# Rows of token moments by TensorE, ScalarE normalisation, two more seven-product pairs and a new product order in the first DFT chunk

## The chip, the cores and the metric

The kernel runs on one core of one Trainium2 chip. A core has TensorE (matrix products), VectorE and ScalarE (elementwise work), GpSimd (small work and the issue of one DMA queue) and SyncE, here called SP, which issues most loads. The metric is the device time of one execution in microseconds (us). All data is float32.

## The reference

For x of 2048 tokens by 512 features, the reference normalises each token, mixes it by a Fourier transform over both axes, and gates the result with a GLU:

```python
xn = (x - mean) / sqrt(var + 1e-5)                       # per token
a, b = xn @ hid_re.T, xn @ hid_im.T                      # along features
s = seq_re @ a - seq_im @ b                              # along tokens
g = silu((sigmoid(xn @ w_gate) * (xn @ w_up)) @ w_down)  # F = 1792
out = x + s * g
```

## The kernel before

**Arithmetic.** Each float32 operand is split into a high part (a rounded copy, made by ScalarE, line 72) and a low part (the rest, by VectorE, line 73). Every product is three matmuls, high by high, high by low and low by high (`mm3`, lines 75 to 78), of 128 weight columns by 512 moving columns. Blocks of two by two products are done with seven products instead of eight, as Strassen and Winograd do: sums and differences of the operands are made first, by VectorE (line 124), and the products are numbered 1 to 7.

**Stages.** A start stage normalises and transposes the first 1024 tokens and does block (0,0) directly. Then come 91 units of gate/up work, seven for each of the 13 pairs (half of the tokens h, group of 256 hidden features g) listed in `BLOCKS`: (0,1) is units 0 to 6, (0,2) is 7 to 13, (0,3) is 14 to 20, (0,4) is 21 to 27, and so on. Unit i of a block runs product 1, 5, 2, 6, 7, 4 or 3 of gate and up (12 matmuls into the PSUM banks ga/ua, gb/ub, gc/uc). The b banks are free from the gate of product 2 until the next block's seed. After it, a unit may run one item of the down projection of the block before: in a pair of class `Plain` there are four items of 12 matmuls, at units 1, 3, 4 and 6 of the block; in a pair of class `Seven` there are seven items of six matmuls, one a unit, the last carried into the next block. Each item ends in `gather`: two copies out of PSUM by ScalarE (line 302) and one DMA of 512 KB that adds into DRAM (line 304, GpSimd's queue). Pair (0,0) has class `Ready`, which is `Plain` with operands made in the start stage. `Plain` holds for h = 0 and g below 3. A `Seven` pair needs weight sums and differences (`Down`: four of 256 columns, one more split) and four sums of its activations.

**Then the transform.** Four chunks along the sequence (`seq_units`), each with seven products of four units in the order `ORDER = (1, 5, 6, 3, 7, 2, 4)`; chunk 0 also runs the last eight down items, one behind every second unit. Products 5, 6, 7 and 4 take sums t1, t2, t3 and t4 of the DFT matrix blocks, products 1, 2 and 3 the blocks themselves. Then the transform along features follows (`hidden_units`).

**Order.** Nothing is reordered by a scheduler. A loop over the units (the last lines of the kernel function) emits, for each unit n: the functions registered with `sooner(n, f)`; the loads that the next five units need; the operands (splits) of the next two units; the unit's matmuls; and the functions registered with `after(n, f)`. Every engine runs its own instructions in that order and waits on semaphores for the others. So an operand split is made two units ahead, behind whatever ScalarE or VectorE was given before it.

**Tokens 1024 to 2047.** They are needed both row by row (normalised and stored to `xn_part`) and turned (features on partitions, raw x_t loaded). `norm_a` makes mean and scale of a tile of 128 tokens: bn statistics on VectorE, three small GpSimd steps (lines 166 to 168). `norm_b` applies them on VectorE (line 173). For the turned form, `turned_half` stores means and scales to DRAM (`m_part`, four DMAs in which each element of 4 bytes goes to its own place, line 183), loads them back broadcast to all partitions, and subtracts and multiplies (line 188). `sums_ahead` makes sums ahead of their use and stores them to DRAM (`w_part`, `s_part`, `t_part`); `t_part` holds t1 to t4 of the first block of chunk 0.

SBUF work tiles come from one pool of 54 pages of 4 KB a partition.

Of the kernel before, what the change touches and what calls it, by code (L numbers as in the profile page):

```python
# [15 lines left out]
P = 128  # L16
# [7 lines left out]
SB = 512  # L24
# [4 lines left out]
FIRST_TURNED = 1, 4  # L29
SEVEN_FROM = 3  # L30
SHARED = 4, 5, 6
# [5 lines left out]
def fnet_glu_kernel(ctx: ExitStack, tc: tile.TileContext, x, x_t, c_re, c_im, w_h, w_gu, w_down, out):  # L37
# [22 lines left out]
    nc.scalar.activation(warm, mhalf, AF.Sigmoid)  # L60
    moments = const.tile([P, 2, KH], F32, name="moments")
    m_part = dram.tile([2, 2, SB], F32, name="m_part")
# [5 lines left out]
    s_part = dram.tile([2, 4, P, 4, D // 2], F32, name="s_part")  # L68
    t_part = dram.tile([1, 4, P, 2, SB], F32, name="t_part")

# [84 lines left out]
    st_of = {}  # L155

    def norm_a(i):
# [3 lines left out]
        nc.vector.bn_stats(st, xs[i])  # L161
        nc.vector.bn_aggr(mv, st)
        mean, scale = mv[:, 0:1], rs[:, 1:2]
        if i >= KH:
            mean, scale = (moments[:, m, i - KH : i - KH + 1] for m in range(2))
            nc.gpsimd.tensor_scalar(mean, mv[:, 0:1], 0.0, None, op0=ALU.add)
        nc.gpsimd.tensor_scalar(rs[:, 0:1], mv[:, 1:2], EPS, None, op0=ALU.add)
        nc.gpsimd.tensor_tensor(scale, rs[:, 0:1], mhalf, op=ALU.pow)
        st_of[i] = mean, scale

    def norm_b(i):
# [3 lines left out]
    def turned_half(n, b, at):  # L175

        both = Load(m_part[b].rearrange("m t -> (m t)").partition_broadcast(P).rearrange("p (m t) -> p m t", m=2), [2, SB])
        raw = [Load(x_t[(2 + b) * 2 + j], [2, SB]) for j in range(2)]

        def store():  # L180
            at = slice(b * SB // P, (b + 1) * SB // P)
            for m in range(2):
                nc.gpsimd.dma_start(m_part[b, m].rearrange("(o p) -> p o", p=P), moments[:, m, at])

        def step(j, m):
            v = xraw[1, j, b] = raw[j].load()
            by = both.load()[:, m, :].unsqueeze(1).to_broadcast([P, 2, SB])
            nc.vector.tensor_tensor(v, v, by, op=(SUB, ALU.mult)[m])

        after(n, store)  # L190
        sooner(at[0] - 2, both.load)
        for i in range(4):
            if i % 2 == 0:
                sooner(at[i] - 4, raw[i // 2].load)
            after(at[i], lambda i=i: step(*divmod(i, 2)))
# [482 lines left out]
    def sums_ahead(make, blocks, to, at, ahead):  # L678

        steps = make(*blocks, to)  # L680

        def step(dst, a, b, op, to):
            v = combine(dst(), a.get(), b.get(), op)
            nc.gpsimd.dma_start(to, v)

        for i, v in zip({diffs: (1, 3, 0, 0), sums: (0, 0, 3, 1)}[make], blocks):
            sooner(at[i] - ahead, v.load)
        for i, v in zip(at, steps):
            after(i, lambda v=v: step(*v))
# [20 lines left out]

    ORDER = (1, 5, 6, 3, 7, 2, 4)
    TURNED = (1, 5, 6, 2, 7, 3, 4)
    SLOT = {1: 0, "a": 0, 2: 1, "b": 1, 3: 2, 5: 3, 7: 4, 6: 5, 4: 6}
# [11 lines left out]

    def seq_units(job):
        ops = a_operands()
# [7 lines left out]
        for tc_ in range(NT):  # L735
# [7 lines left out]
            for pp in range(4):  # L743
                b11, b12, b21, b22 = c_blocks(tc_, pp)
                if tc_ == 0 and pp < 1:
                    t1, t3, t2, t4 = (Load(t_part[pp, i], [2, SB]) for i in range(4))
                else:
                    t1 = Value([b11, b12], onto(b11.load, b12.load, ADD, nc.vector))
                    t2 = Value([b22], onto(t1.get, b22.load, ADD, nc.vector))
                    t3 = Value([b22], onto(b12.load, b22.load, ADD, nc.vector))  # L750
                    t4 = Value([b21], onto(t2.get, b21.load, ADD, nc.vector))
# [92 lines left out]

            for k in ORDER:
                for pp in range(4):
# [129 lines left out]
    with tc.manual_schedule():  # L976
# [4 lines left out]
        for h, g in BLOCKS:  # L981
# [3 lines left out]
            if (h, g) == FIRST_TURNED:  # L985
                turned_at = len(units)
            job = block(h, w, made, job, Seven(h, wd, made) if h or g >= SEVEN_FROM else Plain(h, g), g in SHARED)
        for i in range(0, KH, 2):
            a, b = ((2, 9), (4, 10), (7, 12), (8, 14))[i // 2]
            if i >= 4:  # L990
                sooner(a - 4, lambda i=i: fetch(KH + i))
            for j in (i, i + 1):
                after(a, lambda j=j: norm_a(KH + j))
                after(b, lambda j=j: norm_b(KH + j))
                after(b + 1, lambda j=j: store_xn(KH + j))
        n = turned_at
# [77 lines left out]
```

## Time and profile before

| what | value |
|---|---|
| runs | 810.9, 811.6, 815.87 us; median 811.6 |
| profiled execution | 809.47 us |
| its span | 807.6 us |
| granted TensorE clock | 0.999 |
| DMA | 193.62 MB, mean 240 GB/s |

The span runs from the first to the last instruction. In the profile's lines PE is TensorE, PEld its weight loads, DVE VectorE, ACT ScalarE, POOL GpSimd; L76 is line 76. A group's line gives its busy time and the mean length of one instruction, then the engine's idle time before it and what ended that. In the windows, each line gives the stretch, its length, then for PE, PEld, DVE, ACT and POOL the busy time and the count of instructions, the granted clock, the mean busy share of the DMA engines and GB/s. Timelines give start, length, engine, line and operation, with the idle time before it in brackets. Matmuls overlap in TensorE's pipeline, so their lengths add up to more than the time they take, and a few matmul records are missing from the trace.

### The profile page before, as it was taken

To read this page: it belongs to the slowest core of one execution; us is meant where nothing else is said; L and a number is where in the kernel's file an instruction comes from. 1 tells how busy PE (TensorE), PEld (TensorE's weight loads), DVE (VectorE), ACT (ScalarE), POOL (GpSimd) and SP (SyncE) were. 2 spreads that over 40 slices of the span, in tenths; PEclk is the share of its full clock that TensorE was granted. 3 is DMA by queue.
4 is the path that set the end of the run, shared out by engine and by line. 5 is a ranking of instruction groups with operands and counts; after the bars stand their busy time and mean duration, and the time that the engine had idled before them with its cause. 6 is when DMAs were issued, how large, how long until landed. Compare 5 with 4: busy or idle time off the path is not lost.

```text
span 807.6 us, 10288 instructions
## 1 busy us (share of the span) xinstructions
PE 801.0 (99%) x3630; PEld 665.3 (82%) x3630; DVE 639.7 (79%) x803; ACT 496.9 (62%) x761; POOL 150.8 (19%) x222
## 2 busy tenths in 40 slices
PE   9999999999999999999999999999999999999997
PEld 7988888888888888888888888888888888888886
DVE  6897879876776787787798796888888876986946
ACT  4674657777676678778877765445445545536360
POOL 3146321221222222131211100011101210001201
PEclk9999999999999999999999999999999999999999
DMA  8366994987899998989899988277929994799976
GB/s 278 140 225 110 219 263 72 182 159 156 240 253 226 290 295 236 236 199 175 236 294 311 282 294 293 98 284 286 329 85 324 350 389 141 244 337 386 314 254 104
DMA packets 55651, 193.62 MB, mean 240 GB/s; under 512 B 6320, under 2 KB 6576, under 8 KB 55600
## 3 DMA queue, kind: packets, MB, share of 16 engines
q0 software_dynamic: 24624, 85.48, 45.4%
q1 hardware_dynamic: 30896, 107.43, 37.7%
q8 instruction: 28, 0.46, 0.2%
q14 instruction: 23, 0.19, 0.1%
q10 hardware_dynamic: 80, 0.07, 0.0%
HBM read 110.62 MB, written 85.99 MB: 243 GB/s over the span
## 4 chain that ended last, share of the span: by engine, by line
PE 98%; DMA 1%; DVE 0%; ACT 0%; SPq 0%; issue 0%
PE pd L77 7%; PE pd L76 7%; PE pd L78 7%; PE ga L76 6%; PE ga L77 6%; PE ua L77 6%; PE ga L78 6%; PE ua L78 6%; PE ua L76 6%; PE gc L77 4%; PE uc L77 3%; PE gc L78 3%; PE uc L78 3%; PE gc L76 3%; PE uc L76 3%; PE ub L77 3%
## 5 line engine op out<-in xcount | busy, mean ns | idle before, releaser
L73 DVE TENSOR_TENSOR page<-page 128x1024 fp32r<-128x1024 f32 (+1 forms) x351 | 332.4, 976 | 110.3 <-ACT page L72 109.2
L72 ACT ACTIVATE page<-page 128x1024 fp32r<-128x1024 f32 (+1 forms) x351 | 284.2, 857 | 93.6 <-DVE page L124 74.2
L124 DVE TENSOR_TENSOR page<-page 128x1024 f32<-128x1024 f32 (+2 forms) x216 | 188.8, 893 | 0.9 <-DMA page<-in_w_gu_dram 0.3
L302 ACT ACTIVATE page<-pd 128x512 f32<-128x512 f32 x178 | 104.6, 598 | 67.5 <-PE pd L78 54.6
L304 POOL DMA_DIRECT2D g_part<-page x81 | 71.6, 949 | 282.5 <-ACT page L302 166.4
L76 PE MATMUL pd<-page 128*128 128x512 f32 x234 | 91.0, 389 | 0.0
L77 PE MATMUL pd<-page 128*128 128x512 f32 x234 | 91.0, 389 | 0.0
L78 PE MATMUL pd<-page 128*128 128x512 f32 x234 | 91.0, 389 | 0.0
L76 PE MATMUL ga<-page 128*128 128x512 f32 x200 | 78.2, 391 | 0.0
L77 PE MATMUL ga<-page 128*128 128x512 f32 x200 | 77.9, 389 | 0.0
L76 PE MATMUL ua<-page 128*128 128x512 f32 x200 | 77.8, 389 | 0.0
L77 PE MATMUL ua<-page 128*128 128x512 f32 x200 | 77.8, 389 | 0.0
L78 PE MATMUL ga<-page 128*128 128x512 f32 x200 | 77.8, 389 | 0.0
L78 PE MATMUL ua<-page 128*128 128x512 f32 x200 | 77.8, 389 | 0.0
L76 PEld LDWEIGHTS pd<-page 128*128 128x128 f32 x234 | 43.9, 188 | 9.2
L78 PEld LDWEIGHTS pd<-page 128*128 128x128 f32 x234 | 43.9, 188 | 9.1
L77 PEld LDWEIGHTS pd<-page 128*128 128x128 f32 x234 | 43.9, 188 | 9.1
L77 PE MATMUL gc<-page 128*128 128x512 f32 x124 | 48.3, 390 | 0.0
L76 PE MATMUL gc<-page 128*128 128x512 f32 x124 | 48.2, 389 | 0.0
L78 PE MATMUL gc<-page 128*128 128x512 f32 x124 | 48.2, 389 | 0.0
L76 PE MATMUL uc<-page 128*128 128x512 f32 x124 | 48.2, 389 | 0.0
L78 PE MATMUL uc<-page 128*128 128x512 f32 x124 | 48.2, 389 | 0.0
(133 smaller groups left out, 1302.3 us busy)
## 6 DMA issues: line engine op xcount, KB each, us to landing
g_part<-page POOLq DMA_DIRECT2D x89, 512.0 KB, 8.3
page<-f_part SPq DMA_DIRECT2D x36, 512.0 KB, 6.1
page<-in_c_re_dram SPq DMA_DIRECT2D x34, 512.0 KB, 6.2
page<-in_c_im_dram SPq DMA_DIRECT2D x33, 512.0 KB, 7.0
f_part<-page POOLq DMA_DIRECT2D x28, 512.0 KB, 6.9
page<-in_w_gu_dram SPq DMA_DIRECT2D x22, 512.0 KB, 7.0
page<-xn_part SPq DMA_DIRECT2D x14, 512.0 KB, 5.6
page<-in_w_down_dram SPq DMA_DIRECT2D x11, 512.0 KB, 7.9
```

What stands on the lines that cost most here:

```text
L72: nc.scalar.activation(hi, src, AF.Copy)
L73: nc.vector.tensor_tensor(lo, src, hi.bitcast(F32), op=SUB)
L76: nc.tensor.matmul(ps, ws[0], ms[0], start=first, stop=False, skip_group_check=go_on)
L77: nc.tensor.matmul(ps, ws[0], ms[1], start=False, stop=False, skip_group_check=go_on)
L78: nc.tensor.matmul(ps, ws[1], ms[0], start=False, stop=last, skip_group_check=go_on)
L124: (engine or nc.vector).tensor_tensor(dst, a, b, op=op)
L302: nc.scalar.activation(pg[:, o, :], po, AF.Copy, scale=float(sign))
L304: nc.gpsimd.dma_start(g_part[i], pg, accum_op=ADD)
```

## The change

- Pairs (0,1) and (0,2) become `Seven` pairs: the condition `g >= SEVEN_FROM` becomes `g in SEVENS`, with 1 to 6. Block (0,2) then runs six down items and carries the seventh into (0,3).
- `norm_a` also makes a bias, minus mean times scale (two more GpSimd steps a tile); `second_norm` normalises with one ScalarE instruction in place of `norm_b` on VectorE. The tiles' statistics are made one a unit after units 2 to 9, and they are normalised after units 11, 14, 18 and 22 (before: 9, 10, 12 and 14).
- `turned_half` turns means and scales into rows with one small matmul of TensorE (128 x 8 by the 128 x 128 identity) into a cleared gb bank, copies them out by ScalarE, and stores them by SP as rows of 512 bytes. This stands after units 6 and 13 (before: stores after 4 and 8). The eight subtract and multiply steps stand after units 10 to 13, 17, 18, 22 and 24 (before: 10, 11, 14, 24 and 15, 16, 18, 25).
- In DFT chunk 0 the order is 1, 2, 5, 6, 3, 7, 4. The sums t1 to t4 of its first block stay in their SBUF pages from the time they are made (after units 61, 62, 64 and 66; before: 60 to 63) and are neither stored nor loaded.

```diff
-SEVEN_FROM = 3
+SEVENS = 1, 2, 3, 4, 5, 6
...
-    moments = const.tile([P, 2, KH], F32, name="moments")
+    moments = const.tile([P, 2, 3, 4], F32, name="moments")
+    lines = const.tile([8, P], F32, name="lines")
...
         nc.gpsimd.tensor_tensor(scale, rs[:, 0:1], mhalf, op=ALU.pow)
+        if i >= KH:
+            bias = moment(2, i)
+            nc.gpsimd.tensor_tensor(bias, mean, scale, op=ALU.mult)
+            nc.gpsimd.tensor_scalar(bias, bias, -1.0, None, op0=ALU.mult)
         st_of[i] = mean, scale
+
+    def second_norm(i):
+        nc.scalar.activation(xs[i], xs[i], AF.Identity, scale=moment(1, i), bias=moment(2, i))
...
+        ps = []
+
+        def clear():
+            ps.append(bank("gb")[:8, :P])
+            nc.vector.memset(ps[0], 0.0)
+
         def store():
-            at = slice(b * SB // P, (b + 1) * SB // P)
-            for m in range(2):
-                nc.gpsimd.dma_start(m_part[b, m].rearrange("(o p) -> p o", p=P), moments[:, m, at])
+            columns = moments[:, b, :2, :].rearrange("p m o -> p (m o)")
+            nc.tensor.matmul(ps[0], columns, ident, start=False, stop=True, skip_group_check=True)
+            nc.scalar.activation(lines, ps[0], AF.Copy)
+            nc.sync.dma_start(m_part[b].rearrange("m (o p) -> (m o) p", p=P), lines)
...
+        after(n - 1, clear)
         after(n, store)
-        sooner(at[0] - 2, both.load)
+        sooner(n + 2, both.load)
...
             v = combine(dst(), a.get(), b.get(), op)
-            nc.gpsimd.dma_start(to, v)
+            if isinstance(to, Value):
+                to.at = v
+            else:
+                nc.gpsimd.dma_start(to, v)
...
+    ORDER_FIRST = (1, 2, 5, 6, 3, 7, 4)
...
-                    t1, t3, t2, t4 = (Load(t_part[pp, i], [2, SB]) for i in range(4))
+                    t1, t3, t2, t4 = c_sums
...
-            for k in ORDER:
+            for k in ORDER if tc_ else ORDER_FIRST:
...
-            job = block(h, w, made, job, Seven(h, wd, made) if h or g >= SEVEN_FROM else Plain(h, g), g in SHARED)
+            job = block(h, w, made, job, Seven(h, wd, made) if h or g in SEVENS else Plain(h, g), g in SHARED)
         for i in range(0, KH, 2):
-            a, b = ((2, 9), (4, 10), (7, 12), (8, 14))[i // 2]
+            a, b = ((2, 11), (4, 14), (6, 18), (8, 22))[i // 2]
...
             for j in (i, i + 1):
-                after(a, lambda j=j: norm_a(KH + j))
-                after(b, lambda j=j: norm_b(KH + j))
+                after(a + j - i, lambda j=j: norm_a(KH + j))
+                after(b, lambda j=j: second_norm(KH + j))
...
-        turned_half(4, 0, (n - 18, n - 17, n - 14, n - 4))
-        turned_half(8, 1, (n - 13, n - 12, n - 10, n - 3))
+        turned_half(6, 0, (n - 18, n - 17, n - 16, n - 15))
+        turned_half(13, 1, (n - 11, n - 10, n - 6, n - 4))
...
-        sums_ahead(sums, c_blocks(0, 0), t_part[0], (n + 32, n + 33, n + 34, n + 35), 3)
-        seq_units(job)
+        c_sums = [Value([], None) for _ in range(4)]
+        sums_ahead(sums, c_blocks(0, 0), c_sums, (n + 33, n + 34, n + 36, n + 38), 3)
+        seq_units(job, c_sums)
```

In `turned_half(n, b, at)`, b is the half of the second 1024 tokens; at the call, `n` is 28, the first unit of block (1,4).

More of the change, by code (lines that the diff above doesn't have):

```diff
@@ L68, in fnet_glu_kernel @@
     s_part = dram.tile([2, 4, P, 4, D // 2], F32, name="s_part")
-    t_part = dram.tile([1, 4, P, 2, SB], F32, name="t_part")
     def split(hi, lo, src):
@@ L155, in fnet_glu_kernel, with moment @@
     st_of = {}
+    def moment(m, i):
+        b, o = divmod(i - KH, 4)
+        return moments[:, b, m, o : o + 1]
     def norm_a(i):
@@ L164, in norm_a @@
         if i >= KH:
-            mean, scale = (moments[:, m, i - KH : i - KH + 1] for m in range(2))
+            mean, scale = moment(0, i), moment(1, i)
             nc.gpsimd.tensor_scalar(mean, mv[:, 0:1], 0.0, None, op0=ALU.add)
@@ L724, in silu_ahead, with seq_units @@
         after(n + 3, give)
-    def seq_units(job):
+    def seq_units(job, c_sums):
         ops = a_operands()
```

## The prediction, made before the run

> **What bounds the kernel now.** I read the page first, then the windows by stage, then the timelines of single engines where the change cuts in.
>
> ```profile
> span 807.6 us, 10288 instructions
> ...
> PE 801.0 (99%) x3630; PEld 665.3 (82%) x3630; DVE 639.7 (79%) x803; ACT 496.9 (62%) x761; POOL 150.8 (19%) x222
> ...
> PE 98%; DMA 1%; DVE 0%; ACT 0%; SPq 0%; issue 0%
> ```
>
> TensorE is busy for 99% of the span and carries 98% of the chain of waits. Busy shares flatter a pipelined TensorE, so the next view, TensorE's timeline, is read for the distance between starts:
>
> ```profile
> 99.74 0.39 PE L76 MATMUL uc<-page 128*128 128x512 f32 x1
> ...
> 105.86 0.39 PE L76 MATMUL ub<-page 128*128 128x512 f32 x1
> ```
>
> These two and the 26 rows between them make 27 steps in 6.12 us: 0.227 us a matmul, although each lasts 0.39. That is the price of a matmul added or removed. Windows by stage (DVE, ACT and POOL busy, with counts, behind PE and PEld) tell whether it holds everywhere:
>
> ```profile
> 35.48:65.74 30.26, 30.25 (x135) 24.71 (x134) 26.26 (x39) 19.93 (x33) 12.59 (x23) 1.00 0.45 157
> 65.74:95.66 29.92, 29.92 (x134) 24.77 (x133) 22.61 (x39) 17.16 (x30) 14.20 (x22) 1.00 0.93 159
> 95.66:125.58 29.92, 29.92 (x134) 24.77 (x133) 24.41 (x37) 18.31 (x31) 6.50 (x8) 1.00 0.88 246
> ...
> 452.00:471.00 19.00, 19.00 (x86) 15.63 (x85) 16.69 (x17) 14.60 (x19) 3.13 (x4) 1.00 1.01 306
> ```
>
> The first three are the gate/up blocks (0,1), (0,2), (0,3), whose units start at 0, 7 and 14; the last lies in DFT chunk 0 (rows between are left out). TensorE never rests in them, at full clock. So the only gain to be had is matmuls not run, and any other edit can only cost, by making TensorE wait. VectorE is the next engine, 76 to 88% busy here.
>
> **Twelve matmuls fewer.** A plain pair runs 4 items of 12 matmuls (48), a seven-product pair 7 of 6 (42). Two pairs change: 12 x 0.227 = 2.72 us off TensorE's queue. All of it would reach the end, since TensorE is the chain.
>
> **Two row matmuls more.** Nothing like a plain f32 matmul with 8 weight columns and 128 moving ones is in the trace. The nearest rows, from TensorE's timeline and from the view of line 208, have the same identity and the same width:
>
> ```profile
> 19.09 0.60 PE L208 MATMUL pd<-ident,page 128*128 128x128 f32 x4
> ```
>
> ```profile
> L208 PE MATMUL pd<-ident,page x32: 270/273/476, 6.0 to 27.7; 128*128 128x128 f32 x32
> ```
>
> Four in 0.60 us, the last lasting 0.27, start 0.11 apart. Piped, two cost 0.22 us; if each is exposed for its whole length, 0.55. Below nothing is excluded, since they only add. I take 0.55, because each may stand behind a wait. The Trainium skill (FP8 and Floating Point Precision, TensorE Precision Notes) says that true FP32 takes four passes through the array; as an estimate that would be 4 x 0.11 = 0.44 each, 0.9 in all, and the sum 0.35 us worse. The rows shown are transposes, so they don't decide it.
>
> **What the row matmuls wait for.** They stand after units 6 and 13 in TensorE's own order, so everything behind them (the next block's first product) waits too. The first needs means and scales of token tiles 8 to 11, tile 11 being normalised after unit 5. VectorE reaches that point only after the product of ScalarE's gate of unit 5, which waits for TensorE (rows of the timelines of VectorE, TensorE and GpSimd):
>
> ```profile
> 60.85 0.68 DVE L473 TENSOR_TENSOR page<-page,ua 128x512 f32<-128x512 f32 x1
> ```
>
> ```profile
> 65.74 0.39 PE L76 MATMUL ga<-page 128*128 128x512 f32 x1
> ```
>
> ```profile
> 61.36 0.21 POOL L166 TENSOR_SCALAR moments<-mv 128x1 f32<-128x1 f32 x1
> 61.54 0.20 POOL L167 TENSOR_SCALAR rs<-mv 128x1 f32<-128x1 f32 x1
> 61.82 0.57 POOL L168 TENSOR_TENSOR moments<-rs,mhalf 128x1 f32<-128x1 f32 x1
> ...
> 75.99 1.51 POOL L167 TENSOR_SCALAR rs<-mv 128x1 f32<-128x1 f32 x1
> ```
>
> From 61.5: the new low split of the weight differences (1.2) and the bn statistics (0.7, then a short aggregation) give about 63.6; GpSimd's three steps end 1.0 later when quick, 64.6. Unit 7 starts at 65.74, so 1.1 us is left; a slow GpSimd step like the 1.51 one takes all of it. Stall 0 to 1.2, taken 0.3. The new bias products (two GpSimd steps a tile) come after scale and don't hold the matmul.
>
> The second needs nothing late but the clearing of its bank, put after unit 12 on VectorE, behind a gate product, a 1.2 us split and a 1.2 us subtraction. In that unit a down item now runs, and ScalarE does its gather (two of 0.6 us) ahead of the gate. Counting units 7 to 13 at 12 matmuls plus an item of 6 (none in unit 7), unit 12 ends at 65.74 + 66 x 0.227 + 36 x 0.227 = 88.9 and unit 13 at 92.9. VectorE: gather until 90.1, gate 0.6, product 0.7, split behind its ScalarE half 1.2, subtraction 1.2, clearing about 0.1: 94. So TensorE waits about 1.2 us (0 to 2.5).
>
> **VectorE and ScalarE in blocks (0,1) to (0,3).** Prices by form (groups between are left out):
>
> ```profile
> L73 DVE TENSOR_TENSOR page<-page 128x512 fp32r<-128x512 f32 x161 | 106.2, 686 | 21.4 <-ACT page L72 21.1
> L124 DVE TENSOR_TENSOR page<-page 128x512 f32<-128x512 f32 x84 | 55.9, 686 | 0.6 <-DMA page<-in_w_gu_dram 0.3
> L124 DVE TENSOR_TENSOR page<-page 128x256 f32<-128x256 f32 x32 | 12.8, 420 | 0.3
> L161 DVE BATCH_NORM_STATS2 st<-page 128x6 f32<-128x512 f32 x16 | 10.9, 680 | 2.1 <-DMA page<-in_x_dram 2.0
> L173 DVE TENSOR_SCALAR page<-page,moments 128x512 f32<-128x512 f32 x8 | 4.0, 544 | 0.0
> L188 DVE TENSOR_TENSOR page<-page 128x1024 f32<-128x1024 f32 x8 | 9.8, 1220 | 0.0
> L302 ACT ACTIVATE page<-pd 128x512 f32<-128x512 f32 x178 | 104.6, 598 | 67.5 <-PE pd L78 54.6
> ```
>
> VectorE, busy time per piece (busy over count). Block (0,1): four weight differences 1.6, their low split 1.2, one bn more 0.7: 26.3 becomes 29.8 of 30.3. Block (0,2): six normalisations gone 3.0, one bn gone 0.7, two more subtract/scale steps of the turned half 2.4, four sums 2.7, three more splits 2.0, differences and split 2.8: 22.6 becomes 28.8, in a block that shrinks to 120 x 0.227 = 27.2. Block (0,3): 24.4 - 1.0 - 2.4 + 2.7 + 2.0 = 25.6 of 28.6. So for two blocks VectorE has 58.6 us to do in TensorE's 57.5, and the 1.1 missing must come from the lead it holds at the start of block (0,2):
>
> ```profile
> 43.95 1.22 DVE L73 TENSOR_TENSOR page<-page 128x1024 fp32r<-128x1024 f32 x1
> ...
> 59.65 1.29 DVE L73 TENSOR_TENSOR page<-page 128x512 fp32r<-128x512 f32 x2
> ```
>
> ```profile
> 46.70 0.39 PE L76 MATMUL ga<-page 128*128 128x512 f32 x1
> ```
>
> The operand of unit 7 was done at 60.94, 4.8 us early. 1.1 of 4.8 is bearable, and of the 11.3 us that VectorE idles in the two blocks most is waiting for ScalarE's halves, which a later VectorE finds done. The thin spot is unit 3: its operand ends at 45.17 for 46.70, 1.5 us, and the first differences (0.8) now stand before it. I take 0.3 for thin spots (0 to 3). ScalarE's pieces are of the gather's size, 0.6. Block (0,2): four more gather copies 2.4, three splits 1.8, the differences' split 1.1, two normalisations 1.2: 17.2 becomes 23.7 of 27.2. Block (0,3): six copies 3.6, three splits 1.8, four normalisations 2.4: 18.3 becomes 26.1 of 28.6. Covered, within the same 0 to 3.
>
> **Queues.** SP now issues the stores of the rows and waits there for ScalarE's copy; behind it stand the load of the rows and the next weights. Before, the same place waited longer:
>
> ```profile
> L183 POOL DMA_DIRECT2D m_part<-moments x4: 764/804/863, 62.3 to 80.4; - x4
> ...
> DMA to landing us min/median/max: 12.7/12.8/12.9
> ```
>
> ```profile
> page<-xn_part SPq DMA_DIRECT2D x14, 512.0 KB, 5.6
> ```
>
> The scattered stores took 12.8 us to land for 2 KB. Rows of 512 bytes from 8 partitions should land sooner; the page's list of DMA issues has 5.6 us for far larger transfers. That pays for six more accumulating gathers. On time: nothing. GpSimd's queue loses those four stores (0.8 us each to issue) and four to t_part and gains six gathers; nothing on TensorE but the first row matmul waits for it. The normalised tiles are stored up to eight units later, and their first reader loads after unit 38. The turned half's steps are done by unit 24, before the sum of unit 26 that reads the last of them. Each of these moves costs nothing while that holds, and a wait of VectorE, bounded by rival 2, if not. The four stores to t_part and their loads go; the four pages are held instead from about 300 to 480 us.
>
> **DFT chunk 0.** The four sums stay the same VectorE work. Product 2 needs only splits, so VectorE gains lead in the early products, where down items lengthen TensorE's share; at the end 7 and 4, both with sums to make, now adjoin. Rows of the timelines of VectorE, TensorE and ScalarE:
>
> ```profile
> 468.24 6.90 DVE L73 TENSOR_TENSOR page<-page 128x1024 fp32r<-128x1024 f32 x6
> ```
>
> ```profile
> 470.51 0.39 PE L76 MATMUL ga<-page 128*128 128x512 f32 x1
> ```
>
> ```profile
> 422.38 0.58 ACT L810 ACTIVATE gb<-ga 128x512 f32<-128x512 f32 x1 [1.74 <-PE ga L78]
> ```
>
> After product 3 VectorE must join (two pieces of 512 columns, 1.2 us), then make five pieces of 1.13 (the row's six take 6.90); the last of them, the row's second, ends at 468.24 + 1.13 + 1.22 = 470.59, just when TensorE comes to it at 470.51. In the new order no down item follows product 3 (1.36 us less time), but one sum moves ahead of the join; from 7 to 4 it is join 1.2, sum, two splits 3.5, and about 0.5 carried over, 5.2 for 24 matmuls, 5.4. Taken 0.3 (-0.3 to 1.5). The seed copies that product 2 now waits for start at once, since ScalarE stood idle 1.74 us before them, and a down item (1.36) covers both.
>
> **Sum.** -2.72 + 0.55 + 0.3 + 1.2 + 0.3 + 0.3 = -0.1 us against the profiled execution's 809.47 us (807.6 of span, 1.9 around it): 809.4. The runs shown are 810.9, 811.6 and 815.87, so the profile stands 2.1 below their median. I forecast 810.8, between the lowest run and the median: no change.
>
> **Rivals.**
> (1) *All cover holds.* Against it: the clearing of the bank stands behind a gate by count. For it: TensorE's busy time fills every window shown, so the schedule before kept all its cover. -2.72 + 0.22 = -2.5: 807.0 as in the profile, 809.1 against the median. Chance 0.19.
> (2) *VectorE becomes the bound in blocks (0,1) and (0,2): slower.* If its 11.3 us of idle time (4.0 + 7.3 in the first two windows) stays, because it is set by ScalarE waiting for TensorE unit by unit, it needs 58.6 + 11.3 = 69.9 us for 57.5; less the lead of 4.8 that is a stall of 7.6. It decides once more than 4.8 - 1.1 = 3.7 us of the idle stays. -2.72 + 0.55 + 7.6 = +5.4: 814.9, or 817.0 against the median. Against: most of that idle is one wait for a split that a busy VectorE would overlap. Chance 0.14. By the Trainium skill (TensorE: Matmul & The Clock Gate, Part 1) a TensorE idle for a window of about 3.4 us runs at half clock until warm; were the stall in one piece, that would add an estimated 1.7 us. No window here shows it, the clock being 1.00 throughout.
> (3) *Chunk 0 runs late.* Loads for product 2 come 27 us sooner while DMA is at 1.01 in the window shown. At that window's 306 GB/s a 512 KB load takes 1.7 us; one or two exposed on top of the forecast give 811.1 to 812.8 as in the profile, 813.2 to 814.9 against the median. Against: the t_part loads are gone from the same stretch. Chance 0.08.
> The forecast, with stalls of 1 to 4 us in all, keeps 0.59.
>
> **Numbers.** Range 807.0 to 816.0: from rival 1 in the profile's terms to almost rival 2 at the median. About 1%, 8 us, is what a measurement can tell here from no change. Faster by that would need more than the 12 matmuls give: 0.02. Slower needs rival 2 with 11 us of stall, or 2 and 3 together: 0.07. The rest is 0.91.
>
> **What would show it.** Right: 12 fewer pd matmuls, TensorE's starts 0.227 apart but for a gap near 1 us before the second row matmul and almost none before the first; VectorE over 95% busy in units 0 to 13; rows landing in under 8 us. Wrong: gaps spread over units 7 to 20 whose releaser is VectorE's split (rival 2), gaps at products 5 or 6 after a load (rival 3), or no gap at the second row matmul (rival 1).

## The result and the profile after

The changed kernel takes 815.7 us (median of 22 runs, 814.0 to 818.0) and the kernel before 810.9 us beside it (22 runs, 809.3 to 816.6). The ratio is 1.0047, 95% interval 1.0033 to 1.0062: about 4 us slower, under the 1% that the prediction took as the bound of a change. The time lies at the upper end of the range; the forecast of no movement does not hold, since the interval excludes 1.

The page of the changed kernel:

```profile
span 812.3 us, 10316 instructions
...
PE 800.3 (99%) x3622; PEld 662.5 (82%) x3622; DVE 650.4 (80%) x821; ACT 512.6 (63%) x791; POOL 161.5 (20%) x236
...
PE 87%; DVE 5%; DMA 3%; ACT 2%; issue 2%; SPq 0%; POOL 0%; DVEq 0%; POOLq 0%; ACTq 0%
```

TensorE is still "99% busy", but the chain of waits says more: its share fell from 98% to 87%, so the chain now leaves TensorE. The groups by line show what TensorE and ScalarE were given (busy time and mean ns behind the bar):

```profile
L76 PE MATMUL pd<-page 128*128 128x512 f32 x230 | 89.7, 390 | 0.0
...
L181 ACT ACTIVATE page<-page,moments 128x512 f32<-128x512 f32 x8 | 6.0, 803 | 0.0
...
L200 PE MATMUL gb<-ident,moments 128*8 128x128 f32 x4 | 0.8, 272 | 2.4 <-DVE gb L196 2.4
```

Lines 76, 77 and 78 are 230 each, 690 down matmuls for 702 before: the twelve are gone. Each of the two row matmuls is recorded as two instructions. TensorE's timeline shows where they start and where time is lost (start, length, and in brackets the idle time with what ended it):

```profile
65.57 0.39 PE L78 MATMUL pd<-page 128*128 128x512 f32 x1
65.89 0.39 PE L200 MATMUL gb<-ident,moments 128*8 128x128 f32 x2
66.20 0.50 PE L76 MATMUL ga<-page 128*128 128x512 f32 x1
...
93.31 0.39 PE L78 MATMUL pd<-page 128*128 128x512 f32 x1
96.08 0.38 PE L200 MATMUL gb<-ident,moments 128*8 128x128 f32 x2 [2.38 <-DVE gb L196]
96.39 0.50 PE L76 MATMUL ga<-page 128*128 128x512 f32 x1
...
141.77 0.39 PE L78 MATMUL pd<-page 128*128 128x512 f32 x1
143.07 0.50 PE L76 MATMUL ga<-page 128*128 128x512 f32 x1 [0.91 <-ACT page L475]
...
488.37 0.39 PE L78 MATMUL ga<-page 128*128 128x512 f32 x1
...
489.05 0.39 PE L78 MATMUL ua<-page 128*128 128x512 f32 x1
491.19 0.47 PE L76 MATMUL ga<-page 128*128 128x512 f32 x1 [1.75 <-DVE page L828]
491.50 0.39 PE L77 MATMUL ga<-page 128*128 128x512 f32 x1
```

What a wait costs is counted over two steps from start to start, the one up to the matmul that waited and the one behind it, less 0.227 for each. The second belongs to it because the next matmul, too, starts late, in most cases by 0.11 (0.34 behind the one that waited). There are three large waits:

- **A**, before the second row matmul (end of unit 13): 2.45 us, beside the row's own price.
- **B**, before product 7 of block (0,4) (unit 25): 1.18 us.
- **C**, in DFT chunk 0, between products 7 and 4: 2.00 us.

Two small waits for ScalarE's gathers, near 128 and 132 us, add 0.55. A row matmul costs 0.51 where it waits for nothing (66.20 + 0.34 - 65.57, less 2 x 0.227), 1.02 for both. So -2.72 + 1.02 + 2.45 + 1.18 + 2.00 + 0.55 = +4.5, of the 4.7 us by which the span grew.

Windows by block, (0,1) to (0,4), in the columns of the windows shown of before:

```profile
35.52:65.89 30.37, 30.36 (x135) 24.55 (x133) 28.49 (x45) 20.30 (x33) 15.97 (x28) 1.00 0.42 147
66.20:96.08 29.88, 27.50 (x122) 22.48 (x122) 26.39 (x45) 22.82 (x42) 18.33 (x29) 1.00 0.76 200
96.39:125.08 28.69, 28.69 (x127) 23.75 (x127) 24.20 (x39) 23.17 (x42) 8.15 (x11) 1.00 0.96 227
125.08:153.75 28.67, 27.73 (x120) 22.02 (x119) 26.39 (x39) 23.93 (x43) 8.67 (x11) 1.00 0.94 181
```

VectorE (third pair of numbers) and ScalarE (fourth) are not full in any block. What stops TensorE is the place of a few instructions in their queues.

**Wait A** in VectorE's and **C** in the same timeline:

```profile
92.44 0.69 DVE L493 TENSOR_TENSOR page<-page,ua 128x512 f32<-128x512 f32 x1 [0.67 <-ACT page L490]
93.39 1.23 DVE L73 TENSOR_TENSOR page<-page 128x1024 fp32r<-128x1024 f32 x1 [0.26 <-ACT page L72]
94.53 1.22 DVE L207 TENSOR_TENSOR page<-page 128x1024 f32<-128x1024 f32 x1
95.76 0.17 DVE L196 MEMSET gb<- 8x128 f32 x1
...
488.09 1.22 DVE L124 TENSOR_TENSOR page<-page 128x1024 f32<-128x1024 f32 x1
489.22 1.22 DVE L73 TENSOR_TENSOR page<-page 128x1024 fp32r<-128x1024 f32 x1
490.36 0.68 DVE L828 TENSOR_TENSOR page<-ga,page 128x512 f32<-128x512 f32 x1
```

At A the clearing (line 196) stands behind gate product, split and subtraction, as forecast. At C product 4 adds into the PSUM banks ga and ua in which product 7 has just ended (both belong to chain "a"), so its first matmul must wait until VectorE's join (line 828) has read ga. The last matmul into ga starts at 488.37 (the last three write ua), so ga was complete at about 488.8. The join was held until 490.36, 1.6 us longer: a sum (line 124) and a split (line 73) stand ahead of it in VectorE's order. By the order in which the kernel emits them, they are operands of product 4's third and second unit, so the join was needed before either.

ScalarE's timeline shows why the gate at A was late, and what stands before the copy on which B waits (line 475, `snap`, reads ga after product 6; product 7 writes the same bank):

```profile
88.41 1.51 ACT L181 ACTIVATE page<-page,moments 128x512 f32<-128x512 f32 x2
89.83 1.14 ACT L72 ACTIVATE page<-page 128x512 fp32r<-128x512 f32 x2
90.87 1.06 ACT L322 ACTIVATE page<-pd 128x512 f32<-128x512 f32 x2
91.82 0.59 ACT L490 ACTIVATE page<-ga 128x512 f32<-128x512 f32 x1
...
136.34 1.51 ACT L181 ACTIVATE page<-page,moments 128x512 f32<-128x512 f32 x2
137.75 2.10 ACT L72 ACTIVATE page<-page 128x1024 fp32r<-128x1024 f32 x3
...
141.17 1.36 ACT L72 ACTIVATE page<-page 128x512 fp32r<-128x512 f32 x2
142.44 0.58 ACT L475 ACTIVATE page<-ga 128x512 f32<-128x512 f32 x1
```

Before, the same copy (then line 455) stood here, while product 7 started at 140.54:

```profile
138.67 0.60 ACT L455 ACTIVATE page<-ga 128x512 f32<-128x512 f32 x1
```

It ended 1.3 us early then; in the changed kernel, with product 7 due at 142.00, it ends 1.0 late.

### The profile page after: what moved, and what is told of

Read it like the earlier page. It is cut to its first block, busy times and chain, and to the rows that moved or that the text cites. A ratio compares the mean times of both kernels' runs of the same rounds, so it can differ in the third digit from the quotient of the medians.

```text
span 812.3 us, 10316 instructions
## 1 busy us (share of the span) xinstructions
PE 800.3 (99%) x3622; PEld 662.5 (82%) x3622; DVE 650.4 (80%) x821; ACT 512.6 (63%) x791; POOL 161.5 (20%) x236
## 4 chain that ended last, share of the span: by engine, by line
PE 87%; DVE 5%; DMA 3%; ACT 2%; issue 2%; SPq 0%; POOL 0%; DVEq 0%; POOLq 0%; ACTq 0%
PE pd L78 6%; PE pd L77 6%; PE pd L76 6%; PE ga L76 5%; PE ga L78 5%; PE ua L78 5%; PE ua L76 5%; PE ga L77 5%; PE ua L77 5%; PE ub L78 3%; PE ub L76 3%; PE ub L77 3%; PE gb L78 3%; PE gb L76 3%; PE gb L77 3%; PE gc L77 3%
## 5 line engine op out<-in xcount | busy, mean ns | idle before, releaser
L73 DVE TENSOR_TENSOR page<-page 128x1024 fp32r<-128x1024 f32 (+1 forms) x359 | 338.4, 972 | 108.6 <-ACT page L72 106.2
L72 ACT ACTIVATE page<-page 128x1024 fp32r<-128x1024 f32 (+1 forms) x359 | 290.1, 855 | 99.5 <-DVE page L124 82.1
L124 DVE TENSOR_TENSOR page<-page 128x1024 f32<-128x1024 f32 (+2 forms) x232 | 196.5, 869 | 0.8
L322 ACT ACTIVATE page<-pd 128x512 f32<-128x512 f32 x190 | 110.3, 597 | 47.8 <-PE pd L78 32.3
L324 POOL DMA_DIRECT2D g_part<-page x87 | 76.2, 918 | 283.4 <-ACT page L322 156.8
L76 PE MATMUL pd<-page 128*128 128x512 f32 x230 | 89.7, 390 | 0.0
L77 PE MATMUL pd<-page 128*128 128x512 f32 x230 | 89.5, 389 | 0.0
L78 PE MATMUL pd<-page 128*128 128x512 f32 x230 | 89.5, 389 | 0.0
L76 PEld LDWEIGHTS pd<-page 128*128 128x128 f32 x230 | 43.2, 188 | 9.7 <-ACT page L322 0.9
L78 PEld LDWEIGHTS pd<-page 128*128 128x128 f32 x230 | 43.2, 188 | 9.0
L77 PEld LDWEIGHTS pd<-page 128*128 128x128 f32 x230 | 43.2, 188 | 8.9
```

Of the source, the lines that this page charges most:

```text
L72: nc.scalar.activation(hi, src, AF.Copy)
L73: nc.vector.tensor_tensor(lo, src, hi.bitcast(F32), op=SUB)
L76: nc.tensor.matmul(ps, ws[0], ms[0], start=first, stop=False, skip_group_check=go_on)
L77: nc.tensor.matmul(ps, ws[0], ms[1], start=False, stop=False, skip_group_check=go_on)
L78: nc.tensor.matmul(ps, ws[1], ms[0], start=False, stop=last, skip_group_check=go_on)
L124: (engine or nc.vector).tensor_tensor(dst, a, b, op=op)
```

## The experiments

The theory after the result: the three waits are separate, each is made by one edit of the change, and each goes when that edit alone is undone. The rival: TensorE is held by VectorE or ScalarE as a whole, so that a wait taken away comes back elsewhere. "Lost" in the table is the sum, over all steps of TensorE's timeline from 35 us that are over 0.26 us long, of the step less 0.227.

| kernel | span | lost | median | ratio to before, 95% |
|---|---|---|---|---|
| before | 807.6 | 0.96 | 810.9 | |
| changed | 812.3 | 7.37 | 815.7 | 1.0047 (1.0033 to 1.0062) |
| e1 clearing early | 811.7 | 5.99 | 813.3 | 1.0036 (1.0024 to 1.0048) |
| e2 old order | 810.4 | 5.36 | 813.6 | 1.0036 (1.0023 to 1.0048) |
| e6 both of these | 809.6 | 4.63 | 811.2 | 1.0010 (0.9996 to 1.0023) |
| e3 normalised by VectorE | 812.8 | 7.43 | 814.2 | 1.0056 (1.0036 to 1.0075) |
| e4 e6 with VectorE | 808.5 | 3.37 | 810.4 | 0.9998 (0.9985 to 1.0011) |
| e7 other order | 811.2 | 5.58 | 810.5 | 1.0001 (0.9981 to 1.0021) |
| e10 e6, steps moved | 814.4 | 8.20 | 813.9 | 1.0021 (1.0002 to 1.0040) |
| e9 e6, normalised early | 807.6 | 2.70 | 809.7 | 0.9980 (0.9965 to 0.9995) |
| e13 e6, other places | 807.7 | 2.42 | 810.1 | 0.9990 (0.9977 to 1.0004) |
| e14 e9, sums stored | 808.9 | 3.82 | 810.7 | 0.9998 (0.9985 to 1.0011) |
| e12 e9, scattered stores | 822.6 | 17.73 | 824.5 | 1.0170 (1.0155 to 1.0184) |
| e5 seven products alone | 817.1 | 12.76 | 821.2 | 1.0131 (1.0089 to 1.0173) |

Times were taken on several occasions, so the ratios are what compares them. The medians of e1 to e14 are of 4 to 12 runs each (4 for e5 and e12). Span and lost are of the one profiled execution each.

### Wait A: clear the bank earlier (e1)

```diff
-        after(n - 1, clear)
+        after(n - 3, clear)
```

> The changed kernel with the clearing of the row matmul's bank two units earlier (after units 3 and 10 in place of 5 and 12), nothing else. Theory: the 2.8 us from the start of the last matmul before the second row matmul to the row matmul is only that clearing, late on VectorE's queue; it falls to about 0.3, so the span goes from 812.3 to about 809.8 and the ratio to the kernel before from 1.0047 to about 1.0015; the two other gaps (1.3 us at block (0,4), 2.1 us between products 7 and 4 of chunk 0) stay. Rival (VectorE or ScalarE short of time throughout blocks (0,2) and (0,3)): the lost time comes back as gaps within the next ten units and the span stays above 811.5.

TensorE's timeline:

```profile
94.36 0.39 PE L200 MATMUL gb<-ident,moments 128*8 128x128 f32 x2
```

Wait A is gone: the row matmul starts with no idle time ahead of it. That the clearing made it is shown. Yet lost time fell by 1.4, not 2.45: five waits of 0.15 to 0.33, four for ScalarE's gathers and one for VectorE's additions (line 485), stand between 101 and 132 us, where TensorE now comes earlier. The profiled execution also lost 0.7 in its start stage, ahead of everything changed, so that the span shows only 0.6. Both expectations were partly right: A is one instruction's place, and part of what it cost comes back.

### Wait C: the order in chunk 0 (e2, e7)

```diff
-    ORDER_FIRST = (1, 2, 5, 6, 3, 7, 4)
+    ORDER_FIRST = (1, 5, 6, 3, 7, 2, 4)
```

> The changed kernel with chunk 0 in the old order 1, 5, 6, 3, 7, 2, 4, the sums still kept in SBUF. Theory: product 4 follows product 7 in the same PSUM banks and waits for VectorE's join to read them; with product 2 between, the 2.1 us gap goes, no other of over 0.4 us comes in chunk 0, and the span is about 810.4 (ratio about 1.0025). Rival: chunk 0 is short of VectorE time or of loads in either order, and a gap of over 1 us appears at another product.

The span of the profiled execution came out at 810.4 as expected; the wait between 7 and 4 is gone, A and B stay. The ratio, 1.0036, fell by half of what was expected, with 1.0025 still in its interval. e7 keeps product 2 second and puts product 3 (chain "c") between 7 and 4, with the early clearing:

```diff
-        after(n - 1, clear)
+        after(n - 3, clear)
...
-    ORDER_FIRST = (1, 2, 5, 6, 3, 7, 4)
+    ORDER_FIRST = (1, 2, 5, 6, 7, 3, 4)
```

> The changed kernel with the early clearing, and in chunk 0 the order 1, 2, 5, 6, 7, 3, 4: product 2 stays second, but product 3, whose banks are those of chain c, now stands between 7 and 4, which share the banks of chain a. Bank theory (4 waited until VectorE had joined 7's banks): no wait of more than 0.3 before product 4, though the same sums are still made late; now 6 and 7 adjoin in chain a, so 7 waits for ScalarE's copy of those banks, 0.5 to 1.2 us, a new gap at product 7 in chunk 0. Rival (VectorE simply has too many sums at the end of the chunk, whichever banks): 1 us or more stays before 3 or 4. Span 807.9 plus 0.5 to 1.2 by the bank theory.

No step of TensorE over 0.26 us remains in chunk 0, neither before 4 nor, against the expectation, at 7 behind 6, which also write the same banks. Between those two a down item of 6 matmuls still runs, which the expectation overlooked, and ScalarE's copy of ga (line 821) is done under it. TensorE's timeline (last matmul of 6 into ga, first of 7), and ScalarE's:

```profile
466.25 0.39 PE L78 MATMUL ga<-page 128*128 128x512 f32 x1
...
468.52 0.39 PE L76 MATMUL ga<-page 128*128 128x512 f32 x1
```

```profile
466.68 0.60 ACT L821 ACTIVATE page<-ga 128x512 f32<-128x512 f32 x1 [1.78 <-PE ga L78]
```

A reader that is on time starts 0.43 us after the start of the last matmul into its bank, while ua is still written. This one ends at 467.28; without the down item, 7 would have been due at 467.16. VectorE's timeline at the join of 3:

```profile
489.80 0.69 DVE L828 TENSOR_TENSOR page<-page,gc 128x512 f32<-128x512 f32 x1 [0.43 <-PE gc L78]
```

VectorE makes the same sums for the chunk, and here it waits for TensorE before the join of 3 (line 828). So C was not the early place of product 2, nor too much VectorE work for the chunk. It takes two things together: a join that is late, and a next product in the banks that it reads. e2 and e7 both remove the two at once, so how they share the 2.00 us is not shown by a run; moving the join ahead of the sum and the split was not tried. The profiled execution of e7 lost 2.2 elsewhere, near 226 us, where ScalarE waited for a gather's transfer; e6 shows the same with 1.3, the others do not.

### Wait B: ScalarE's normalisation, or its place (e3, e10, e9)

```diff
-                after(b, lambda j=j: second_norm(KH + j))
+                after(b, lambda j=j: norm_b(KH + j))
```

> The changed kernel with the second half's normalisation back on VectorE, at the new places. Theory: ScalarE's two normalisations of 0.8 us each are what made its copy late at product 7 of block (0,4): that gap of 1.3 us goes, and the gap before the second row matmul shrinks by 0.5 to 1.5 us, as ScalarE's gather ahead of it comes sooner, less 1.1 for VectorE's own two normalisations; span 810.5 to 811.3. Rival: ScalarE was late for its gathers and splits anyway; the 1.3 us gap stays.

B did not go (product 7 starts 1.58 us after its neighbour, 1.30 in the changed kernel), although ScalarE had 1.5 us less to do in unit 22. A shrank by 0.6; a new wait for the copy of line 475 came at 318 us (1.03 between starts). That ScalarE's longer instruction by itself makes B is out. e10 moves two subtract and scale steps of 1.2 us away from units 22 and 24, on top of early clearing and old order:

```diff
-        turned_half(13, 1, (n - 11, n - 10, n - 6, n - 4))
+        turned_half(13, 1, (n - 11, n - 10, n - 9, n - 3))
```

> The changed kernel with the early clearing and the old order in chunk 0; ScalarE normalises where the changed kernel does, but the last two steps of the second turned half go from units 22 and 24 to 19 and 25. Theory T (VectorE is late at unit 25 by the 1.2 us subtraction of unit 22): the wait before product 7 of block (0,4) falls to under 0.3. Theory L with the normalisations as the cause: it stays within 0.3 of the 1.1 lost. Both the early clearing and the old order together should leave a span of 812.3 - 2.5 - 1.9 = 807.9 by L, 806.8 by T.

B stays at 1.28 between starts, so the subtraction of unit 22 doesn't make it either. The test is not clean: the load of x that belongs to the moved steps came three units sooner, and in the profiled execution VectorE then waited 3.7 us for weights near 116 us, which cost TensorE 2.3. e9 moves the normalisations instead, still on ScalarE:

```diff
-            a, b = ((2, 11), (4, 14), (6, 18), (8, 22))[i // 2]
+            a, b = ((2, 9), (4, 10), (6, 12), (8, 14))[i // 2]
```

> The changed kernel with the early clearing, the old order in chunk 0, and ScalarE's normalisations at units 9, 10, 12 and 14 (where VectorE had them before) in place of 11, 14, 18 and 22. Theory L: the wait before product 7 of block (0,4) falls from 1.1 us lost to under 0.4; span 807.6 - 2.7 + 0.6 = 805.5 plus 0 to 0.7 of small waits; ratio about 0.9975. Rival S: it stays at 0.8 or more, span 806.8 or more. A third way: ScalarE, which then normalises in units 9 to 14, is late there instead, and waits of 0.3 us each appear in block (0,2); then the span is about the same as by S, but with no gap near 141 us.

ScalarE's timeline of e9 (product 7 of block (0,4) starts without a wait):

```profile
83.69 1.54 ACT L181 ACTIVATE page<-page,moments 128x512 f32<-128x512 f32 x2
85.11 1.16 ACT L72 ACTIVATE page<-page 128x512 fp32r<-128x512 f32 x2
86.15 0.61 ACT L475 ACTIVATE page<-ga 128x512 f32<-128x512 f32 x1
```

and the one larger wait that is left, in TensorE's:

```profile
86.81 0.50 PE L76 MATMUL ga<-page 128*128 128x512 f32 x1 [0.94 <-ACT page L475]
```

B is gone, on the same engine and with the same instructions: it was where the normalisations were put. Late in blocks (0,3) and (0,4) they hold the splits, which hold VectorE, which holds ScalarE's copies in turn. That ring was read from the timelines; which of the four pairs weighs most in it was not tried. In their early places one pair still stands right ahead of a copy of line 475 (unit 10 before unit 11), and makes a wait of the kind of B. With the three edits undone or replaced, lost time and span are both 4.7 us below the changed kernel's: A, B and C, 5.6 together, and the two small waits are gone, and 1.2 came back at 86.8 us and 0.3 at 81.5. e9 has the lowest ratio, 0.998 of the time before (0.9965 to 0.9995). Only the runs together show that 0.2%: the profiled spans of e9 and of the kernel before are both 807.6.

### Putting the fixes together (e4, e6, e13)

e6 is early clearing and old order, e4 those and VectorE's normalisation.

> The changed kernel with the early clearing and the old order in chunk 0 and nothing else: the two gaps of 2.5 and 1.9 us go, the one before product 7 of block (0,4) stays with 1.1 lost, small waits of ScalarE's gathers (0.2 to 0.3 each) come in blocks (0,2) and (0,3). If the gaps simply add up: span 812.3 - 2.5 - 1.9 + 0.5 = 808.4, ratio 1.000. Rival (a TensorE that isn't stopped early meets ScalarE and VectorE later, so that half of what is gained is lost again): 810 or more, ratio 1.002.

> All three edits together: early clearing, old order, normalisation on VectorE. Theory of three separate waits: what is left is 12 matmuls fewer, 2.7 us, against two row matmuls of 0.31 each: span about 807.6 - 2.7 + 0.6 + 0.3 = 805.8, ratio about 0.998. Rival of a VectorE short of time: VectorE has 4 us more again, gaps of over 1 us in units 7 to 20, span above 808.

e6 regained 2.7 of the 4.4 us of A and C; the span lies between the two expectations, and 1.3 of what is missing is the wait near 226 us named above. e4 ends level with the kernel before, 2.7 us over what was expected of it, with B at 1.56 between starts. The span of its rival was met (over 808), but not by the rival's sign: no step over 1 us came in units 7 to 20. e13 places the normalisations of e6 behind units 11, 12, 14 and 15:

```diff
-            a, b = ((2, 11), (4, 14), (6, 18), (8, 22))[i // 2]
+            a, b = ((2, 11), (4, 12), (6, 14), (8, 15))[i // 2]
```

> As the run with the normalisations put back (early clearing, old order in chunk 0), but with ScalarE's pairs of normalisations after units 11, 12, 14 and 15: none of these stands right before the unit whose ScalarE copy of the banks of chain a (snap) TensorE waits for, which are the units 10, 11, 17 and 18. Theory Q (1.6 us of ScalarE work queued ahead of a snap shows as a gap at the next product in the same banks; elsewhere it is hidden): the gap of 1.33 us at 85.5 us goes, none over 0.4 comes in its place, the one near 141 us stays away; span 805.5 to 806.2, ratio about 0.996. Rival (ScalarE has no room for the normalisations in block (0,2) at all): 1 us or more is lost in units 12 to 17; span 807 or more.

The wait at 85 us went as expected and B fell to 0.2, but 0.67 was lost at 110.9 us, again for the copy of line 475, and 0.33 at 101 us. The span of 807.7 is above the 805.5 to 806.2 that theory Q gave; the rival's span was met, and about 1 us was lost, 0.3 in its units 12 to 17 and 0.7 just behind them. The result cannot be told from e9. Keeping the pairs from standing right ahead of a copy was not enough: the wait at 110.9 stands before unit 18, three units behind the last pair, and ScalarE's timeline has no pause from that pair, at 105.84, to the copy, at 111.05.

### The parts by themselves (e5, e12, e14)

e5 is the kernel before with the two seven-product pairs and nothing else.

```diff
-SEVEN_FROM = 3
+SEVENS = 1, 2, 3, 4, 5, 6
```

> The kernel before with one edit: gate/up blocks (0,1) and (0,2) get the seven-product pairs; normalisations, rows, order of chunk 0 and stored sums stay as before. Theory L (block (0,4) is late in the changed kernel because normalisations and subtract/scale steps were moved into units 14 to 25): here they stay early, so no wait of more than 0.5 us before product 7 of block (0,4); span 807.6 - 2.7 = 804.9, ratio about 0.9966. Rival S (the seven items a block, with their gathers and splits, make ScalarE and VectorE late by themselves): the wait stands there with 0.8 us or more although nothing was moved, and others appear in blocks (0,1) to (0,3); span 806 or more.

Each expectation was half right: no wait stands before product 7 of block (0,4), as theory L had it, but waits came in blocks (0,2) and (0,3) and a span far over 806, as rival S had it. The twelve matmuls less come with the largest loss but one, 1.3% slower than before. TensorE's timeline:

```profile
86.64 0.39 PE L78 MATMUL pd<-page 128*128 128x512 f32 x1
90.87 0.79 PE L76 MATMUL ga<-page 128*128 128x512 f32 x1 [3.85 <-ACT page L455]
```

ScalarE's, and GpSimd's:

```profile
90.22 0.60 ACT L455 ACTIVATE page<-ga 128x512 f32<-128x512 f32 x1 [4.17 <-DMA g_part<-page]
```

```profile
90.70 1.83 POOL L304 DMA_DIRECT2D g_part<-page  x2 [9.29 <-DMA g_part<-page]
```

ScalarE's copy waits for a page that an accumulating gather still reads, and GpSimd stands 9.3 us because the next gather adds to a place whose last gather has not landed. The scattered stores of means and scales (line 183, at 79.6 us) stand just ahead of that; what share they have in the late landing was not tried. Two more waits, at 80.7 and 118.1 us, are again for line 455. So, in the places where the kernel before has its other work, the two pairs by themselves do not pay.

e12 is e9 with the scattered stores in place of the rows, at the units of the rows:

```diff
-            columns = moments[:, b, :2, :].rearrange("p m o -> p (m o)")
-            nc.tensor.matmul(ps[0], columns, ident, start=False, stop=True, skip_group_check=True)
-            nc.scalar.activation(lines, ps[0], AF.Copy)
-            nc.sync.dma_start(m_part[b].rearrange("m (o p) -> (m o) p", p=P), lines)
+            for m in range(2):
+                nc.gpsimd.dma_start(m_part[b, m].rearrange("(o p) -> p o", p=P), moments[:, b, m, :])
...
-        after(n - 3, clear)
```

> The run with the normalisations put back, with GpSimd's scattered stores of means and scales in place of TensorE's rows, at the same units 6 and 13 (no clearing, no row matmuls). Theory G (the scattered stores hold up the accumulating gathers behind them on GpSimd's queue, and a ScalarE copy then waits for the buffer that a gather still reads, as in the kernel with the seven products alone): a gap of 2 us or more in units 8 to 17 whose ScalarE copy was released by a g_part transfer; span 809 or more, so that the rows pay for their 0.6 us. Rival: the scattered stores are hidden here too, and the span falls by the rows' 0.6 us to 807.0.

15.0 us more span than e9. The rows are worth far more than the 0.6 us that they were thought to cost, but not for the expected reason: the wait is not on gathers but on loads. VectorE's timeline:

```profile
94.30 0.69 DVE L124 TENSOR_TENSOR page<-page 128x512 f32<-128x512 f32 x1 [4.67 <-DMA page<-in_w_gu_dram]
```

SP's timeline shows why the weights are late; first e12, then e9:

```profile
81.83 0.33 SPq L87 DMA_DIRECT2D page<-m_part  x1
...
82.73 1.16 SPq L87 DMA_DIRECT2D page<-in_w_gu_dram  x2
```

```profile
67.28 0.35 SPq L202 DMA_DIRECT2D m_part<-lines  x1
69.43 0.35 SPq L87 DMA_DIRECT2D page<-m_part  x1
...
70.34 0.87 SPq L87 DMA_DIRECT2D page<-in_w_gu_dram  x2
```

The load of means and scales waits on SP until their stores have landed, and the weights stand behind it. The rows let it go 2.2 us after their store; the scattered stores take 11.3 us (median) to land, and GpSimd issues the first of them only at 71.1. So the same load and the same weights come 12.4 us later: 3.8 for the later issue and 8.6 for the longer way from store to load. TensorE loses 5.9 us at 90.7 and 4.5 at 127.9; most of the rest is its clock behind these two waits (last section).

The comparison holds for these units: in the kernel before, the stores stand at units 4 and 8 and the loads later behind them.

e14 is e9 with the four sums of chunk 0 stored and loaded as before, at their old units:

```diff
-        sums_ahead(sums, c_blocks(0, 0), c_sums, (n + 33, n + 34, n + 36, n + 38), 3)
+        sums_ahead(sums, c_blocks(0, 0), t_part[0], (n + 32, n + 33, n + 34, n + 35), 3)
...
-                    t1, t3, t2, t4 = c_sums
+                    t1, t3, t2, t4 = (Load(t_part[pp, i], [2, SB]) for i in range(4))
```

> The run with the normalisations put back, with the four sums of chunk 0 stored to DRAM and loaded again as in the kernel before, at their old units. The forecast (keeping them in SBUF costs and gains nothing): span within 0.4 of 807.6, the same ratio within the interval. Rivals: the stores and loads cost DMA time that shows, 1 us more; or the four pages held in SBUF had made other buffers late, and it is 0.5 to 1 us faster.

ScalarE's timeline at the start of chunk 0:

```profile
436.23 1.06 ACT L73 ACTIVATE page<-page 128x1024 fp32r<-128x1024 f32 x1 [2.74 <-DMA page<-t_part]
```

In the profiled execution the load of a sum comes late and TensorE loses 0.9 at 437.6 us; the span grows by 1.3. The intervals of the two ratios overlap, so the 0.2% between them is not established. Before, no such wait is in TensorE's timeline.

## Why the prediction failed, step by step

- **Twelve matmuls fewer, -2.72:** right, by the count of 690 and the 0.227 between starts.
- **Row matmuls, 0.55:** 1.02 measured. The matmul itself was near (0.31 from its start to the next). Not in the sum were the next matmul's late start behind it (0.11) and the row's own late start (0.32 behind its neighbour, where 0.227 is usual). The latter is no wait: the same 0.32 stands before the second row in e1, whose bank was cleared 8 us before. The estimate of 0.44 each from the Trainium skill (FP8 and Floating Point Precision, TensorE Precision Notes), four passes for true FP32, lies between the 0.31 and the whole cost of 0.51; the trace records two instructions a row and does not show passes.
- **First row, 0.3:** no wait is seen. But GpSimd ended the last scale only at 65.64, not at 64.6, 0.25 before the row started.
- **Second row, 1.2:** right mechanism, short by half; 2.45, at the end of its bound. (The count of matmuls up to the end of unit 12 should read 72 and 30 for 66 and 36; their sum is right.) The reckoning put the clearing's end at 94 and it came at 95.9. It left out the two normalisations of unit 11, which stand ahead of unit 12's splits, gather and gate on ScalarE, 1.5 us; the prediction counted them only in a block's sum of busy time. It also priced them as gathers, 0.6; they take 0.80. The Trainium skill (ScalarE: Activation LUTs, What ACT_TABLE_LOAD costs) states about 93 ns more for each scale or bias that is read per partition; as an estimate, 0.60 + 2 x 0.093 = 0.79, which agrees with the 0.803 here.
- **"Covered, within the same 0 to 3":** the step that failed for B. VectorE's and ScalarE's sums by block were not too low (26.4 and 22.8 in block (0,2), 24.2 and 23.2 in (0,3), all under the forecast), and unit 3 had no wait. But a sum by block does not see the one instruction that TensorE waits for: a copy that frees ga, due within one down item of 1.36 us. The prediction stopped at block (0,3), and B is in (0,4), where normalisation was moved to.
- **DFT chunk 0, 0.3 (-0.3 to 1.5):** the step that failed for C, 2.00, beyond its bound. "From 7 to 4 it is join 1.2, sum, two splits 3.5" compares VectorE's work with TensorE's time, and for the operands that was right. It forgot that 4 adds into the banks that the join of 7 reads, so that the join is due not within 24 matmuls but before 4's first. It came 1.6 us after it could have started, behind a sum and a split that were less urgent. An estimate for a join on time: from the start of the last matmul into ga it is 0.43 to the join's start (e7), 0.68 for the join and 0.15 to the restart (as here), 1.26 in all, where four steps of 0.227 are free, 0.91. So the shared bank would have cost some 0.35 us even then, near the 0.3 that the prediction took for other reasons, which is luck; the late join brought the other 1.6.
- **Queues, "on time: nothing":** right that the rows land sooner (2.2 us from store to load in e9). But against scattered stores at the same units they are worth 15 us (e12), and this term was never priced.
- **Rivals:** (1) needed all cover to hold, and three places did not. (2) VectorE was 94 and 88% busy in the first two blocks, not over 95%, and bounded neither. (3) No wait for a load showed at products 5 or 6. The time of (2) was nearly met, by other ways.

In all the sum of -0.1 lacked 4.6 of the 4.8 us between it and the span: C 1.7, A 1.25, B 1.18, and half a microsecond each from rows and small waits, less the 0.6 that the prediction had set aside and that did not show.

## What to carry to other kernels

Where TensorE never rests, list for every moved product which PSUM banks it writes and who must have read them, before counting operand work: between two neighbours in one bank, whatever stands ahead of the reader in its own queue stops TensorE (1.6 us here), and another product or a down item between them covers it. Work that is moved to another engine should be placed by the next deadline in that engine's queue (here ScalarE's copies that free a bank), and not by the engine's busy share of a block. An edit that removes matmuls can depend on the rest of a change: price it alone too, here 1.3% slower alone and level with the kernel before, or 0.2% faster by the runs, with the others well placed.

## What the hardware did that was not expected

TensorE's clock falls after a long wait, and it did so in two of the kernels. Windows of e5 around its longest wait (the granted clock is the third number from the end):

```profile
87.00:90.87 3.87, 0.03 (x1) 0.00 (x0) 3.14 (x6) 0.65 (x2) 0.17 (x1) 0.85 0.50 100
90.87:96.00 5.13, 5.13 (x12) 4.07 (x13) 4.21 (x6) 2.97 (x6) 5.13 (x7) 0.50 0.96 204
```

After 4.2 us between starts, twelve matmuls take 5.13 us at half the clock, where 12 x 0.227 = 2.7 would do: 2.4 us beyond the wait itself. In e12 the same follows both of its long waits, and the slow steps add 2.6 and 1.7 us. The 2.77 of wait A left the clock at 1.00. The Trainium skill (TensorE: Matmul & The Clock Gate, Part 1) gives about 3.4 us of idle time as the window. By the length of the waits the cases lie on either side of it. The fall itself came sooner in e5: a mean of 0.85 over 3.87 us, if the clock was either 1.00 or 0.50, puts it 1.2 us before the end of the wait, about 2.7 after the last matmul's end.
